# A spectral layer and a two-level mixture of experts on one core: rows of a pair in half tiles, two buffers for z tiles and weights, one hand-given order for early and main jobs

## The chip, the cores and the metric

One Trainium2 chip, one of its cores. The metric is device microseconds of one launch. The kernel before took 1245.92 us, the median of three runs from 1244.65 to 1246.6.

## The reference

`x` has 8 batches of 1856 positions and 256 channels. Each batch goes through a Fourier layer, and each of the 14848 resulting rows through one of 16 small networks, chosen in two levels.

```python
X = np.fft.rfft(x, axis=1);  Xr, Xi = X.real, X.imag
Yr = Xr @ w_r - Xi @ w_i + b_r
Yi = Xr @ w_i + Xi @ w_r + b_i
Y  = shrink(Yr) + 1j * shrink(Yi)          # sign(v) * max(|v| - 0.01, 0)
y  = np.fft.irfft(Y, n=1856, axis=1).reshape(14848, 256)

g  = argmax(y @ w_group);      e = argmax(y @ w_expert[g])     # 4 groups of 4 experts
out[row] = softmax_g * softmax_e * (relu(y @ w1[g, e]) @ w2[g, e])   # 256 -> 1024 -> 256
```

## The kernel before, in words

**Numbers.** fp32 operands are split into a high and a low fp32r part, and a product is three matmuls: high by high, high by low, low by high. The high part is a copy on ACT, the low part a subtraction on DVE. So nearly every matmul on PE waits for an ACT step and a DVE step.

**Spectral part.** The batches go in four pairs (0 to 3). 1856 = 29 x 64, so a transform is a DFT over 29, a DFT over 64 with its twiddles, and on the way back the same in reverse. A pair's spectrum stands in a "z tile" (`zys[pr]`, 32 KB per partition), its output rows in a row tile (`vs[pr]`, 128 partitions x 32 rows x 260 numbers: 256 channels, a row id and the gate).

**Routing.** For each half of a pair (16 rows per partition) PE computes 20 logits per row (`g_mm`), and a chain of small DVE steps (`route_g`) finds the expert, the gate, and the slot in that expert's list. The 32 rows per partition then go to the lists in DRAM (`xs_d`) by 32 indirect DMAs, the scatters: they are issued on POOL (L274), and the next one waits until the one two before it has landed (`FLY = 2`).

**Experts.** Eight *early jobs* (`EJOBS`: experts 0 to 3, two lists of 256 rows each) run while the last pair is finished; their rows are fetched as soon as the pairs before have been scattered. Their weights come through the staging tiles `xt` and are split into an 8192-number weight tile. Then come the *main jobs* (`JOBS`) for the rest of each list, with rows fetched by `fetch` (L435, L294 and L295 for the row ids and gates), prepared by `prep` (L446, L449, L450) and multiplied by `up_g` (L462 to L468) and `down_g` (L516, L517). A row's result is stored by an indirect DMA on POOL (L503).

**What sets the order.** PE, ACT and DVE run in the order in which the program emits their instructions (`tc.manual_schedule`). Up to the end of the early jobs this order is a string, `ORDER`, in which each letter emits the next instance of one step; DMAs go to SP's and POOL's queues in the same order. The letters that matter here, with the engine:

- `l` loads a piece of x of pairs 2 and 3 or of an early expert's weights (SP, L570 and L575); `c` first DFT (PE, L581); `d` transpose into the z tile (DVE, L343); `e` second DFT (PE, L595); `f g i` copies and signs (ACT), `h` remainder (DVE, L613); `j` bias (ACT); `k` the complex linear layer, 24 matmuls (PE, L638); `m n` two relus (ACT, L645); `o` their difference into the z tile (DVE, L651), which ends the forward work of a pair;
- `p q` high and low part (ACT L549, DVE L553), `r` first inverse DFT (PE, L320), `s` 16 transposes per pair into the row tile (DVE, L677); `t u` high and low part of rows, `v` second inverse DFT (PE), `w` its result back into the row tile (ACT, L700), `x` rows turned (PE, L708), `y z` copies into a `yt` tile (ACT or DVE, L714), `G` gate logits (PE, L731), `H` their transpose (DVE, L739), `R` one routing step (DVE), `S` one scatter (POOL, L274);
- `W V` split of an early expert's weights (ACT L760, DVE L765), `F` fetch of early rows (SP, L774), `I` their ids, `T X Y` turned and split (PE, ACT L790, DVE L795), `U` first layer (PE, L807), `A B` relu and remainder (ACT L814, DVE L818), `D` second layer (PE), `E J` gating (ACT L836, DVE L841), `K` the store (POOL, L503).

**Buffers.** The pool `big` has three tiles of 32.5 KB per partition. z tiles, row tiles, x of pair 1, and the split weights of the early and main jobs take turns in them; whoever takes a tile waits for the last reader of what stood there. So a pair's first `s` (which takes a tile) waits until an older row tile or z tile is done with.

**The two schedules.** `ORDER` is emitted inside one `manual_schedule`, the main jobs inside a second one. Between them the pools of the main jobs are opened (`xq`, `yp`, `hq`, two PSUM pools, `ft`) and the table of flexible jobs is begun.

Of the kernel before, what the change touches and what calls it, by code (L numbers as in the profile page):

```python
# [31 lines left out]
K1 = 15  # L32
# [30 lines left out]
RRSkRRhSidRdfkdgShnmioSjRcRnRcmRRSjclRokRRSdddScncmdojcSdeldSfehgcfihSgcidcdcSdkdlSeSnkmfoSgjhieSnkmfoSgjhpipe
qSmqkfghSpiqpneqSmojkfSghnijoeSmknfojghiemrnrfsgjrsrpspepskphiqqrqmqrsfgrsprpsepnskpjhiqqrqfqgrsprpsrpsepskhiq
qrqfqgrsrsrseskhtioutmuetovtumuvwvwxtwxuyzxtvtzuvwutvwuvwtvwuxwxyxyxyxtzGtzuGtufvHgvnRRwvuRwhvRwRRjeRRwRxRixtR
RxtukRtRRRtRRRyRRyRRyvfgxuwRzRnvRjGRwRRkRRRShiuuvSfovwhmeowSxmxzgyeSinxxnojzmSzcjoGndSjcoHcRRdSRcRdclRdScRRcdR
RcdSRklRRRdSRRRRRRRRSkmRRnfdjShgcmocSndcfojghReSdiiRcdRScRlRcRRkSRRdddScmcnSdfkojldgShiemSnkfojShgiemSnkfojShg
# [88 lines left out]
def spectral_moe(ctx: ExitStack, tc: tile.TileContext, x, wri, bri, wgate, w1, w2, cst, out):  # L156
# [4 lines left out]
    big = ctx.enter_context(tc.tile_pool(name="big", bufs=3))  # L161
# [52 lines left out]
    def route_g(pr, L, r0, n):  # L214
# [47 lines left out]
        for r in range(n):  # L262
            pend.append((pr, sloti[:, r:r + 1], vs[pr][:, r0 + r, :]))
# [37 lines left out]
    inv = ctx.enter_context(ExitStack())  # L301
# [900 lines left out]
```

## Time and profile before

| what | value |
|---|---|
| three runs, median (lowest to highest) | 1245.92 us (1244.65 to 1246.6) |
| the profiled execution, its own time | 1245.95 us |
| its span in the trace | 1243.8 us |
| mean granted clock of PE | 0.983 |
| busy: PE, PE weight loads | 1182.3 us (95%), 1018.1 us (82%) |
| busy: DVE, ACT, POOL | 750.3, 670.1, 255.3 us |
| early and spectral part, main jobs | 580.6, 663.2 us of the span |

PE, PEld (its weight loads, beside the matmuls), DVE, ACT and POOL are engines; SPq is SP's DMA queue. In a timeline row stand the start and the duration in us, engine, line, operation, out<-in by the program's tile names, and in brackets the us that the engine waited just before it and what ended that wait. `big` in a row is whatever tile of that pool the line uses. In a row of waits stand the engine, tile and line that waited, what released it, the us waited, the number of waits and the longest one. A busy share is an average over stages with different limits, so the stages are read one by one.

### The profile page before, as it was taken

What the parts mean: (1) busy time and instruction counts of PE and PEld (TensorE: products, weight loads), DVE (VectorE), ACT (ScalarE), POOL (GpSimd) and SP (SyncE); (2) the same over time, 40 slices, a digit from 0 to 9 for tenths busy, and PEclk for the clock granted to TensorE, in tenths of its full rate; (3) what the DMA queues carried; (4) which work ended last, traced back from release to release, by engine and by line L of the source; (5) the groups of instructions that cost most, each with busy time, mean ns of one, the idle gap of its engine ahead of it and who ended that gap; (6) DMA issues with size and microseconds to landing.
All of it is one profiled execution on the core that took longest, in us unless ns stands there. A gap on an engine that the chain in (4) does not pass through costs nothing.

```text
span 1243.8 us, 20312 instructions
## 1 busy us (share of the span) xinstructions
PE 1182.3 (95%) x7418; PEld 1018.1 (82%) x7418; DVE 750.3 (60%) x1678; ACT 670.1 (54%) x1512; POOL 255.3 (21%) x257
## 2 busy tenths in 40 slices
PE   8999999999999789939999999999999999999997
PEld 5988988886999378938879888798798888888876
DVE  4459765878598868624655645555555474474452
ACT  2876967584869266414354544445454463463442
POOL 1000054014402534541101111111111211211111
PEclk9999999999999999979989999999999999999999
DMA  9870034005100243431325345345243345346200
GB/s 382 338 291 23 2 111 143 9 13 185 65 1 21 75 163 120 162 117 41 120 102 174 120 167 179 108 138 212 83 148 120 116 165 188 108 143 226 95 13 28
DMA packets 38629, 155.89 MB, mean 125 GB/s; under 512 B 7285, under 2 KB 9466, under 8 KB 28032
## 3 DMA queue, kind: packets, MB, share of 16 engines
q1 hardware_dynamic: 19648, 104.45, 24.1%
q0 software_dynamic: 12048, 30.67, 6.8%
q10 hardware_dynamic: 6832, 19.46, 4.0%
q8 instruction: 59, 0.97, 0.3%
q14 instruction: 42, 0.34, 0.1%
HBM read 104.60 MB, written 52.46 MB: 126 GB/s over the span
## 4 chain that ended last, share of the span: by engine, by line
PE 80%; ACT 5%; DMA 4%; issue 4%; DVE 4%; POOL 1%; POOLq 0%; SPq 0%; DVEq 0%; ACTq 0%
PE ph L462 21%; PE py L516 15%; PE pw L638 11%; PE py L517 8%; PE bank L320 6%; PE pg L595 3%; PE bank L581 2%; PE ph L807 2%; PE bank L708 2%; DMA big<-in_x_dram 2%; PE pg L446 2%; PE ph L481 2%; DMA xs_d<-big,sloti 1%; PE bank L731 1%; PE ph L1040 1%
## 5 line engine op out<-in xcount | busy, mean ns | idle before, releaser
L516 PE MATMUL py<-big,hh 128*128 128x512 f32 x824 | 298.5, 402 | 0.0
L462 PE MATMUL ph<-xth,big 128*128 128x384 f32 (+1 forms) x896 | 256.4, 361 | 2.0 <-DVE yo L841 1.1
L503 POOL DMA_INDIRECT out_dram<-yo,si x123 | 121.2, 985 | 596.6 <-DVE yo L524 515.2
L517 PE MATMUL py<-big,hl 128*128 128x256 f32 x824 | 231.8, 281 | 0.9 <-DVE hl L468 0.9
L274 POOL DMA_INDIRECT xs_d<-big,sloti x128 | 130.8, 1022 | 367.2 <-ACT yt L714 133.8
L468 DVE SCALAR_TENSOR_TENSOR hl<-ph,hh 128x256 fp32r<-128x256 f32 x448 | 151.7, 381 | 68.7 <-ACT hh L466 68.3
L516 PEld LDWEIGHTS py<-big,hh 128*128 128x128 f32 x824 | 155.0, 188 | 37.7 <-issue 3.2
L462 PEld LDWEIGHTS ph<-xth,big 128*128 128x128 f32 x896 | 165.8, 189 | 20.9 <-PE ph L462 1.8
L466 ACT ACTIVATE hh<-ph 128x256 fp32r<-128x256 f32 x448 | 134.3, 353 | 78.2 <-PE ph L462 74.4
L523 ACT ACTIVATE yo<-py,si 128x256 f32<-128x256 f32 x103 | 48.9, 475 | 218.5 <-PE py L517 218.5
L462 PE MATMUL ph<-xtl,big 128*128 128x384 f32 (+1 forms) x448 | 161.0, 359 | 0.0
L517 PEld LDWEIGHTS py<-big,hl 128*128 128x128 f32 x824 | 154.9, 188 | 1.6 <-DVE hl L468 1.5
L524 DVE SCALAR_TENSOR_TENSOR yo<-py,si,yo 128x256 f32<-128x256 f32 x103 | 49.8, 484 | 176.0 <-ACT yo L523 176.0
L638 PE MATMUL pw<-wh,xh 128*128 128x256 f32 x480 | 121.9, 293 | 0.0
L638 PE MATMUL pw<-wl,xh 128*128 128x256 f32 x480 | 115.8, 280 | 0.0
L422 DVE TENSOR_TENSOR big<-xt,big 128x512 fp32r<-128x512 f32 x168 | 114.1, 683 | 0.0
L421 ACT CAST big<-xt 128x512 fp32r<-128x512 f32 x168 | 104.1, 624 | 0.0
L638 PEld LDWEIGHTS pw<-wh,xh 128*128 128x128 f32 x480 | 90.4, 188 | 2.7 <-issue 2.1
L638 PEld LDWEIGHTS pw<-wl,xh 128*128 128x128 f32 x480 | 90.5, 189 | 1.9 <-issue 1.7
L462 PEld LDWEIGHTS ph<-xtl,big 128*128 128x128 f32 x448 | 84.7, 189 | 7.2
L553 DVE TENSOR_TENSOR sl<-big,sh 128x512 fp32r<-128x512 f32 x112 | 73.1, 693 | 18.5 <-ACT sh L549 18.2
L549 ACT CAST sh<-big 128x512 fp32r<-128x512 f32 x112 | 66.3, 626 | 22.4 <-DVE big L677 10.4
(202 smaller groups left out, 2009.1 us busy)
## 6 DMA issues: line engine op xcount, KB each, us to landing
xt<-in_w_dram SPq DMA_DIRECT2D x50, 1024.0 KB, 5.2
xs_d<-zero ACTq DMA_DIRECT2D x16, 1170.0 KB, 6.3
big<-in_w_dram SPq DMA_DIRECT2D x16, 1024.0 KB, 9.1
big<-in_x_dram SPq DMA_DIRECT2D x8, 1024.0 KB, 13.0
xt<-in_x_dram SPq DMA_DIRECT2D x8, 1024.0 KB, 5.4
xg<-xs_d SPq DMA_DIRECT2D x16, 390.0 KB, 3.2
xg<-xs_d SPq DMA_DIRECT2D x12, 520.0 KB, 4.7
xg<-xs_d SPq DMA_DIRECT2D x8, 260.0 KB, 4.1
```

Of the source, the lines that this page charges most:

```text
L274: ins = nc.gpsimd.indirect_dma_start(out=xs_d, out_offset=bass.IndirectOffsetOnAxis(ap=sl_, axis=0), in_=row, in_offset=None, bounds_check ...
L320: nc.tensor.matmul(o, lhsT=lhs[a_], rhs=rhs[b_], start=i == 0, stop=i == 2)
L421: nc.scalar.copy(out=wt[:, 2 * i, cs], in_=raws[i][:, cs])
L422: nc.vector.tensor_tensor(out=wt[:, 2 * i + 1, cs], in0=raws[i][:, cs], in1=wt[:, 2 * i, cs].bitcast(F32), op=ALU.subtract)
L462: nc.tensor.matmul(o[:, :n], lhsT=a_[:, ch, fs], rhs=b_[:, ch, 0:n], start=k == 0, stop=k == 5)
L466: nc.scalar.activation(out=hh[:, f, :m], in_=ov, func=AF.Relu)
L468: nc.vector.scalar_tensor_tensor(out=hl[:, f, :m], in0=ov, scalar=0.0, in1=hh[:, f, :m].bitcast(F32), op0=ALU.max, op1=ALU.subtract)
L503: ins = nc.gpsimd.indirect_dma_start(out=out, out_offset=bass.IndirectOffsetOnAxis(ap=ids.si[:, t:t + 1], axis=0), in_=ysb, in_offset=None ...
L516: nc.tensor.matmul(o, lhsT=hh[:, f, ts], rhs=w2b[:, :, f, :], start=f == 0, stop=f == 7, skip_group_check=True)
L517: nc.tensor.matmul(o[:, 0:D], lhsT=hl[:, f, ts], rhs=w2h[:, f, :], start=False, stop=f == 7, skip_group_check=True)
L553: nc.vector.tensor_tensor(out=lo, in0=src, in1=units[key].bitcast(F32), op=ALU.subtract)
L638: nc.tensor.matmul(y[:, bt * D:(bt + 1) * D], lhsT=a_[:, bt * 2 + ch, cs], rhs=w_[:, ri, ch, :], start=False, stop=fin, skip_group_check=True)
```

## The change

**Row tiles.** `big` has two tiles instead of three, for z tiles and weights only. The rows of all pairs live in one tile `v` of three half tiles (16 rows per partition each). A pair uses two of them: half 0 is always the first, half 1 the second for pairs 0 and 2 and the third for pairs 1 and 3. So a pair's rows come to stand on the first half of the pair before, but on the second half of the pair two before. x of pair 1 is loaded into the last two thirds of `v` before any rows are there. The transposes of step `s` therefore write two runs of 16 instead of one of 32 in a row (for odd pairs the two are not adjacent).

**Smaller tiles.** A `yt` tile holds 4 row groups instead of 8, so `G` is called 32 times instead of 16, each with eight matmuls half as wide. The hidden tiles of the early jobs hold 2 of the 8 feature blocks instead of all 8, with 6 buffers of each name for 2.

**One order.** One `manual_schedule` (`ms`) now holds both `ORDER` and the main jobs. The pools of the main jobs are opened with `reuse_waits="tile"`. Weights of main jobs take turns in `third` (a pool of one tile opened after the spectral part) and the two tiles of `big`.

**The string.** `ORDER` is a new string, 2040 letters for 2024 (16 more `G`); the steps are the same and each kind keeps its own sequence. Of its 19 lines the diff shows the last.

```diff
-AYBDSUEJUKABDASBUSUABDSABDESJDKDEJKDDEJKDEJK
+BDASBUEJSUDXSYDAASBBDEJSUUASBDASBUEJSUKDDAKABBDKDEJKDEJDKEJK
...
-    big = ctx.enter_context(tc.tile_pool(name="big", bufs=3))
+    big = ctx.enter_context(tc.tile_pool(name="big", bufs=2))
...
+    vv = vp.tile([128, 3, 16, RW], F32, name="v")
+    vs = {pr: vv[:, 0:2] if pr % 2 == 0 else vv[:, 0:3:2] for pr in range(NP)}
...
     def load_x(pr):
-        t = big.tile([128, 4, 32, 64], F32, name="big")
+        if pr:
+            t = vv.rearrange("p s r w -> p (s r w)")[:, 16 * RW:16 * RW + 8192].rearrange("p (c r d) -> p c r d", c=4, r=32)
+        else:
+            t = big.tile([128, 4, 32, 64], F32, name="big")
...
     def split_w(raws):
-        wt = big.tile([128, 4, 2048], F32R, name="big")
+        wt = next(homes).tile([128, 4, 2048], F32R, name="big")
...
     def b_turn(pr, j):
-        if j == 0:
-            vs[pr] = big.tile([128, 32, RW], F32, name="big")
-        nc.vector.transpose(out=vs[pr][:, :, j * 16:(j + 1) * 16].rearrange("p r d -> p d r"),
+        nc.vector.transpose(out=vs[pr][:, :, :, j * 16:(j + 1) * 16].rearrange("p h r d -> p d h r"),
                             in_=psum.pop(("b", pr, j)).rearrange("p (k d b) -> p d k b", k=16, b=2))
...
-        if u % 4 == 0:
-            yts[pr, u // 4] = wi.tile([128, 2, 8, 128], F32, name="yt", bufs=2)
+        if u % 2 == 0:
+            yts[pr, u // 2] = wi.tile([128, 2, 4, 128], F32, name="yt", bufs=2)
...
-    @steps_of(pairs, range(4))
+    @steps_of(pairs, range(8))
     def g_mm(pr, h):
...
-        cs = slice(h % 2 * 256, h % 2 * 256 + 256)
+        cs = slice(h % 4 * 128, h % 4 * 128 + 128)
...
-        if f == 0:
-            hid[n] = [early["hp"].tile([128, 8, 256], F32R, name=nm) for nm in ("hh", "hl")]
+        hid[n, f] = [early["hp"].tile([128, 2, 256], F32R, name=nm) for nm in ("hh", "hl")]
...
+    ms = ExitStack()
     with ExitStack() as ph:
         done = 0
-        with tc.manual_schedule(engines=engines):
-            for c in ORDER.replace("\n", ""):
-                next(steps[c])
+        ms.enter_context(tc.manual_schedule(engines=engines))
+        for c in ORDER.replace("\n", ""):
+            next(steps[c])
...
-                    early["hp"] = ph.enter_context(tc.tile_pool(name="hp", bufs=2))
+                early["hp"] = ph.enter_context(tc.tile_pool(name="hp", bufs=6))
...
+    homes = cycle((pool("third", 1), big, big))
...
-    with tc.manual_schedule(engines=engines):
+    with ms:
         prev = None
```

Lines move by one to fourteen: L274 becomes L275, L294 and L295 become L295 and L296, L450 becomes L457, L574/L575 become L581/L582, L677 becomes L685, L774 becomes L782, L795, L818 and L841 become L803, L825 and L848.

The instruction order shows where the change moves work. First DVE at the end of the early jobs. L818 and L841 are remainders and gatings of early jobs, L795 an early job's row remainder, L294 and L295 the ids of a main job's rows, L450 the remainder of its turned rows. Before:

```order
531 L818 SCALAR_TENSOR_TENSOR hl<-ph,hh 128x512
532 L294 TENSOR_SCALAR si<-xg 128x3
533 L795 TENSOR_TENSOR xtl<-pg,xth 128x512
534 L295 COPY si<-xg 128x3
535 L818 SCALAR_TENSOR_TENSOR hl<-ph,hh 128x512
536 L450 TENSOR_TENSOR xtl<-pg,xth 128x2x256
537 L818 SCALAR_TENSOR_TENSOR hl<-ph,hh 128x512 x2
538 L841 SCALAR_TENSOR_TENSOR yo<-bank,si,yo 128x256 x2
539 L450 TENSOR_TENSOR xtl<-pg,xth 128x2x128
```

The same place after:

```order
542 L803 TENSOR_TENSOR xtl<-pg,xth 128x512
543 L825 SCALAR_TENSOR_TENSOR hl<-ph,hh 128x512 x2
544 L848 SCALAR_TENSOR_TENSOR yo<-bank,si,yo 128x256
545 L825 SCALAR_TENSOR_TENSOR hl<-ph,hh 128x512 x2
546 L848 SCALAR_TENSOR_TENSOR yo<-bank,si,yo 128x256
547 L825 SCALAR_TENSOR_TENSOR hl<-ph,hh 128x512 x2
548 L848 SCALAR_TENSOR_TENSOR yo<-bank,si,yo 128x256 x3
549 L295 TENSOR_SCALAR si<-xg 128x3
550 L296 COPY si<-xg 128x3
551 L457 TENSOR_TENSOR xtl<-pg,xth 128x2x256
552 L457 TENSOR_TENSOR xtl<-pg,xth 128x2x128
```

The main job's ids and row remainders (128x3, 128x2x256, 128x2x128) stood between the early jobs' last steps and now stand behind all of them.

Second, SP's queue, which issues the loads: `xt<-in_w_dram` are halves of an expert's weights, `xg<-xs_d` rows from the lists (520 numbers per partition for an early job, 780 for a main job). Before:

```order
13 L575 DMA xt<-in_w_dram 128x2048 x2
14 L774 DMA xg<-xs_d 128x520 x7
15 L575 DMA xt<-in_w_dram 128x2048 x2
16 L774 DMA xg<-xs_d 128x520
17 L575 DMA xt<-in_w_dram 128x2048 x4
18 L409 DMA xt<-in_w_dram 128x2048
19 L435 DMA xg<-xs_d 128x780
```

And after:

```order
12 L582 DMA xt<-in_w_dram 128x2048 x2
13 L782 DMA xg<-xs_d 128x520
14 L582 DMA xt<-in_w_dram 128x2048 x2
15 L782 DMA xg<-xs_d 128x520 x6
16 L582 DMA xt<-in_w_dram 128x2048 x2
17 L782 DMA xg<-xs_d 128x520
18 L582 DMA xt<-in_w_dram 128x2048 x2
19 L416 DMA xt<-in_w_dram 128x2048 x2
20 L442 DMA xg<-xs_d 128x780 x3
```

The second expert's weights stood behind seven fetches of early rows and now stand behind one; the first main weights (L416) stand ahead of the first main rows as two, where one was ahead before.

Third, DVE where the steps `s` of pair 1 begin (L677, then L685), with `q` (L553, then L560), `h` (L613, L620), `o` (L651, L658) and pair 2's `d` (L343, L350) around them. Before:

```order
173 L677 STREAM_TRANSPOSE big<-bank 128x16x32 x4
174 L613 TENSOR_TENSOR xl<-pg,xh 128x4x128
175 L553 TENSOR_TENSOR sl<-big,sh 128x512 x4
176 L677 STREAM_TRANSPOSE big<-bank 128x16x32 x4
177 L613 TENSOR_TENSOR xl<-pg,xh 128x4x128
178 L553 TENSOR_TENSOR sl<-big,sh 128x512 x4
179 L677 STREAM_TRANSPOSE big<-bank 128x16x32 x4
```

After:

```order
163 L560 TENSOR_TENSOR sl<-big,sh 128x512 x4
164 L685 STREAM_TRANSPOSE v<-bank 128x16x2x16 x3
165 L560 TENSOR_TENSOR sl<-big,sh 128x512 x3
166 L685 STREAM_TRANSPOSE v<-bank 128x16x2x16 x3
167 L560 TENSOR_TENSOR sl<-big,sh 128x512 x4
168 L620 TENSOR_TENSOR xl<-pg,xh 128x4x128
169 L685 STREAM_TRANSPOSE v<-bank 128x16x2x16
170 L620 TENSOR_TENSOR xl<-pg,xh 128x4x128
171 L560 TENSOR_TENSOR sl<-big,sh 128x512 x2
172 L685 STREAM_TRANSPOSE v<-bank 128x16x2x16
```

The transposes have the same count and size, with their output in two pieces, and stand more singly among the other steps.

More of the change, by code (lines that the diff above doesn't have):

```diff
@@ L1 @@
 from contextlib import ExitStack
-from itertools import islice
+from itertools import cycle, islice
 import numpy as np
@@ L63 @@
[L63 to L67, printed above, removed]
@@ L229, in route_g @@
         rs = slice(r0, r0 + n)
-        nc.vector.reciprocal(out=vs[pr][:, rs, D + 1:RW], in_=se.unsqueeze(2).broadcast_to([128, n, RW - D - 1]))
+        nc.vector.reciprocal(out=vs[pr][:, h, :, D + 1:RW], in_=se.unsqueeze(2).broadcast_to([128, n, RW - D - 1]))
         yield
-        nc.vector.tensor_scalar_add(out=vs[pr][:, rs, D], in0=kc("GID")[:, rs], scalar1=float(pr * PAIR))
+        nc.vector.tensor_scalar_add(out=vs[pr][:, h, :, D], in0=kc("GID")[:, rs], scalar1=float(pr * PAIR))
         yield
@@ L262, in route_g @@
         for r in range(n):
-            pend.append((pr, sloti[:, r:r + 1], vs[pr][:, r0 + r, :]))
+            pend.append((pr, sloti[:, r:r + 1], vs[pr][:, h, r, :]))
         yield
@@ L681, in p_high @@
     def p_high(pr, u):
-        high(("p", pr, u), vs[pr][:, 2 * u:2 * u + 2, 0:D])
+        high(("p", pr, u), rows2(pr, u))
     @steps_of(pairs, u16)
     def p_low(pr, u):
-        rest(("p", pr, u), vs[pr][:, 2 * u:2 * u + 2, 0:D])
+        rest(("p", pr, u), rows2(pr, u))
     @steps_of(pairs, u16)
@@ L743, in route_steps @@
             for h in range(2):
-                yield from route_g(pr, logits[pr, h], h * 16, 16)
+                yield from route_g(pr, logits[pr, h], h)
             if pr == NP - 3:
@@ L827, in down_mm @@
         for f in range(half * 4, half * 4 + 4):
-            last.append(nc.tensor.matmul(o, lhsT=hid[n][0][:, f, ts], rhs=w2b[:, :, f, :], start=f == 0, stop=f == 7,
-                                         skip_group_check=True))
-            nc.tensor.matmul(o[:, 0:D], lhsT=hid[n][1][:, f, ts], rhs=w2h[:, f, :], start=False, stop=f == 7,
+            hh, hl = hid[n, f // 2 * 2]
+            nc.tensor.matmul(o, lhsT=hh[:, f % 2, ts], rhs=w2b[:, :, f, :], start=f == 0, stop=f == 7, skip_group_check=True)
+            nc.tensor.matmul(o[:, 0:D], lhsT=hl[:, f % 2, ts], rhs=w2h[:, f, :], start=False, stop=f == 7,
                              skip_group_check=True)
@@ L853, in spectral_moe @@
         Y=e_low, U=up_mm, A=up_high, B=up_low, D=down_mm, E=down_act, J=down_add, K=down_out)
+    ms = ExitStack()
     with ExitStack() as ph:
         done = 0
[L857 to L867 removed]
+        ms.enter_context(tc.manual_schedule(engines=engines))
+        for c in ORDER.replace("\n", ""):
+            next(steps[c])
+            done += c == "o"
+            if c == "o" and done == NP * K1:
+                fwd.close()
+                early["mp"] = ph.enter_context(tc.tile_pool(name="mp", bufs=1))
+                yp.append(ph.enter_context(tc.tile_pool(name="yp", bufs=3)))
+                early["hp"] = ph.enter_context(tc.tile_pool(name="hp", bufs=6))
+                early["pp"] = ph.enter_context(tc.tile_pool(name="pp", bufs=2, space=PSUM))
+                early["py"] = ph.enter_context(tc.tile_pool(name="py", bufs=1, space=PSUM))
         assert not pend and all(next(g, None) is None for c, g in steps.items() if c not in "yzS")
@@ L1011, in half_load @@
     def half_load(k):
-        wt = big.tile([128, 4, 2048], F32, name="big")
+        wt = next(homes).tile([128, 4, 2048], F32, name="big")
         starts = []
```

80 lines of the change are left out of this document (41 added, 39 removed).

## The prediction

> **What bounds the kernel now.** I read the stages first: busy time of each engine between the places where one pair's forward work ends and the next stage begins (columns: stretch in us and its length, busy us and instructions of PE, PEld, DVE, ACT, POOL, then granted clock, DMA share, GB/s).
>
> ```profile
> span 1243.8 us, 20312 instructions
> ...
> 22.50:87.60 65.10, 64.86 (x498) 60.05 (x499) 26.74 (x41) 47.81 (x92) 0.00 (x0) 1.00 0.82 320
> 87.60:204.00 116.40, 115.03 (x830) 97.53 (x829) 89.36 (x166) 81.74 (x160) 23.30 (x24) 1.00 0.25 85
> 204.00:315.30 111.30, 107.32 (x790) 91.75 (x789) 86.30 (x161) 76.42 (x150) 28.73 (x29) 1.00 0.21 70
> 315.30:408.80 93.50, 89.02 (x729) 82.57 (x728) 75.40 (x143) 73.44 (x145) 21.62 (x22) 1.00 0.08 29
> 408.80:457.80 49.00, 43.77 (x238) 28.79 (x239) 39.02 (x65) 23.81 (x46) 24.29 (x24) 0.93 0.27 91
> 457.80:466.50 8.70, 3.48 (x24) 3.01 (x22) 2.66 (x10) 2.65 (x6) 0.39 (x1) 0.81 0.77 299
> 466.50:529.50 63.00, 62.67 (x472) 57.61 (x472) 46.30 (x107) 33.06 (x65) 30.08 (x28) 0.97 0.42 141
> 529.50:549.00 19.50, 0.56 (x3) 0.19 (x1) 2.45 (x7) 1.94 (x4) 11.70 (x12) 0.64 0.36 123
> 549.00:580.60 31.60, 31.55 (x205) 28.99 (x205) 10.67 (x21) 8.76 (x17) 5.85 (x6) 0.95 0.19 68
> 580.60:1243.80 663.20, 644.51 (x3576) 557.68 (x3576) 359.55 (x945) 316.33 (x825) 106.03 (x108) 0.99 0.37 129
> ```
>
> Two things stand out. From 580.6 on, the main jobs keep PE busy (644.5 of 663.2), and the change leaves them as they are. Before that there are 580.6 us in which PE is mostly busy but with two holes: 457.8 to 466.5 (3.5 us busy of 8.7, clock 0.81) and 529.5 to 549.0 (0.6 of 19.5, clock 0.64). The waits of PE up to 582 us name what ended them:
>
> ```profile
> PE ph L807 <- DVE xtl L795: 15.5, 1, 15.5
> PE bank L708 <- ACT big L700: 5.5, 2, 5.3
> ...
> PE ph L807 <- DVE hl L818: 3.5, 1, 3.5
> ```
>
> The timeline of the larger hole shows who held DVE:
>
> ```profile
> 530.82 0.47 ACT L836 ACTIVATE yo<-bank,si 128x256 f32<-128x256 f32 x1 [3.43 <-DMA out_dram<-yo,si]
> ...
> 542.07 0.98 POOL L274 DMA_INDIRECT xs_d<-big,sloti  x1 [0.30 <-issue]
> ...
> 544.66 0.33 SPq L435 DMA_DIRECT2D xg<-xs_d  x1
> ...
> 548.23 0.17 DVE L294 TENSOR_SCALAR si<-xg 128x3 int32<-128x3 f32 x1 [15.22 <-DMA xg<-xs_d]
> 548.31 0.68 DVE L795 TENSOR_TENSOR xtl<-pg,xth 128x512 fp32r<-128x512 f32 x1
> ...
> 549.05 0.58 PE L807 MATMUL ph<-xtl,big 128*128 128x256 f32 x1 [15.54 <-DVE xtl L795]
> ...
> 551.35 0.41 PE L807 MATMUL ph<-xth,big 128*128 128x256 f32 x1
> ```
>
> si<-xg 128x3 is the index step of the first **main** job (three row groups; the early jobs have two). It waits for rows that are fetched only once the last scatter (542.07) has landed, and it stands in DVE's queue ahead of the split (L795) and the relu remainders of early jobs whose data are there. DVE sits still for 15.2 us with early work behind it, and PE with it.
>
> The smaller hole is a load that left late:
>
> ```profile
> 452.80 2.72 SPq L774 DMA_DIRECT2D xg<-xs_d  x6
> 455.62 1.06 SPq L575 DMA_DIRECT2D xt<-in_w_dram  x2
> ...
> 463.85 1.66 ACT L760 CAST big<-xt 128x512 fp32r<-128x512 f32 x3 [6.06 <-DMA out_dram<-yo,si]
> ```
>
> SP issues the second early expert's weights after six fetches of early rows, and those wait for pair 2's scatters. ACT reaches the split of these weights at 457.8 and starts at 463.85; the releaser named is a store, but this cast needs the load issued at 455.62. The copies of pair 3 behind it on ACT are what PE waits for (L700, 5.3).
>
> **The change part by part.** *One hand-given order through early and main jobs.* In the new program all of DVE's early work stands ahead of the first main index step. The 15.5 us go. The 3.5 us ahead of them come from ACT waiting 3.43 for a staging buffer whose store is in POOL's queue between scatters; that can come back, so I count half. Restarting was slow: ten L807 starts from 549.05 to 551.35 take 2.30 us, 0.23 each, where PE's usual distance is 0.1175 (48 of L638 in 5.64, below), so 1.1 more. Together 15.5 + 1.7 + 1.1 = 18.3 gained. The Trainium skill, "TensorE: Matmul & The Clock Gate", Part 1, has the array at half clock after an idle window, until some 3.4 us of work have passed; by that the restart would cost about 1.7 (an estimate from the page) and the sum below would be 0.6 larger; the row's 1.1 is used.
>
> What is late next: the first main job's preparation, formerly done between early matmuls, now follows the last early matmul.
>
> ```profile
> 552.41 0.59 ACT L449 CAST xth<-pg 128x512 fp32r<-128x512 f32 x1 [19.66 <-PE pg L446]
> ...
> 553.04 0.69 DVE L450 TENSOR_TENSOR xtl<-pg,xth 128x512 fp32r<-128x512 f32 x1 [3.38 <-ACT xth L449]
> ```
>
> Cast 0.59, remainder 0.69 and the remainder of the third row group (half as wide, 0.4) leave PE some 1.7 us of waiting; before it waited about 0.7 less there. Its rows must be there too: from 542.07 (last scatter) to 548.23 (rows used) are 6.2 us. By the terms here the early jobs end at about 580.6 - 32 = 549, so scatters that end no sooner than before cost 1 to 2 more. I take +3 for the boundary (1 to 8).
>
> *SP's order.* In the new order the second expert's weights are issued ahead of the six fetches. The hole of 8.7 - 3.5 = 5.2 goes; I take 5 (2 to 5.2; a load can still be late, never earlier than its buffer).
>
> *The order string.* All letters are the same steps, differently mixed. For each piece of 40 letters I added up each engine's time, and took the largest engine per piece, averaged over where the pieces begin. A letter of DVE or ACT costs its group's mean; one of PE its matmuls times their distance in an unbroken run. Rows that carry most of it (groups by line: count, busy us, mean ns, idle before; chain: start, us, count):
>
> ```profile
> 42.55 5.64 PE pw L638 x48
> ...
> 251.83 3.67 PE bank L320 x30
> ...
> L677 DVE STREAM_TRANSPOSE big<-bank 128x512 f32<-128x512 f32 x48 | 48.2, 1122 | 7.8 <-DMA xs_d<-big,sloti 7.7
> L645 ACT ACTIVATE rn<-pw,nlam,CF 128x512 f32<-128x512 f32 x60 | 46.9, 785 | 15.0 <-PE pw L638 11.4 <-DVE big L343 3.4
> L553 DVE TENSOR_TENSOR sl<-big,sh 128x512 fp32r<-128x512 f32 x112 | 73.1, 693 | 18.5 <-ACT sh L549 18.2
> ```
>
> So one k (24 matmuls) is 2.82 us of PE, one s 1.12 of DVE, one q 0.69. Up to the last forward step of pairs 0, 1, 2, 3, the sheet gives 62.2, 123.1, 116.7, 103.3 for the old string, in all 405.3; the four stages above took 65.1 + 116.4 + 111.3 + 93.5 = 386.3. For the new string it gives 69.8, 110.1, 106.7, 106.2, in all 392.8. The difference of 12.5, at 386.3/405.3, is 11.9 gained (0 to 14; pieces of 20 or 80 letters give 14 and 10). For the rest of the string it gives 144.8 and 146.6: 1.8 lost.
>
> *Half tiles.* A pair's 16 transposes into its rows (s) now need only the first 16 scatters of the pair before, but the new string puts s close behind them. How fast POOL scatters, beside loads of x (first rows) and in a stretch where DVE has nothing but transposes (last two, nine distances apart):
>
> ```profile
> 185.75 0.97 POOL L274 DMA_INDIRECT xs_d<-big,sloti  x1 [1.64 <-DVE big L343]
> 189.46 0.97 POOL L274 DMA_INDIRECT xs_d<-big,sloti  x1 [2.73 <-DMA xs_d<-big,sloti]
> 190.74 0.98 POOL L274 DMA_INDIRECT xs_d<-big,sloti  x1 [0.30 <-issue]
> 195.48 0.97 POOL L274 DMA_INDIRECT xs_d<-big,sloti  x1 [3.77 <-DMA xs_d<-big,sloti]
> ...
> 201.21 0.97 POOL L274 DMA_INDIRECT xs_d<-big,sloti  x1 [3.48 <-DMA xs_d<-big,sloti]
> ...
> 414.87 0.97 POOL L274 DMA_INDIRECT xs_d<-big,sloti  x1 [4.94 <-DMA xg<-xs_d]
> ...
> 429.21 0.98 POOL L274 DMA_INDIRECT xs_d<-big,sloti  x1 [0.30 <-issue]
> ```
>
> Undisturbed, one takes (429.21 - 414.87)/9 = 1.59 us, and a load of x adds about 3. From a pair's first scatter to the next pair's first s the new string holds 32.3, 27.5 and 33.7 us of PE letters, some 10% more in real time: 36, 30, 37. Sixteen scatters and a landing of about 2.6 (544.66 less 542.07) need 28, plus 12 for four loads of x in pair 0 and 3 for one in pair 1: 40, 31, 28. DVE waits 4 + 1 + 0; I take 5 (0 to 15). Behind the waiting s on DVE stand the splits that PE's next matmuls need, so it counts in full. For odd pairs the transpose writes two pieces of 16 instead of 32 in a row; the nearest rows are 1122 ns (these) and 704 (the forward transposes), so 32 of them cost 0, at most 32 x 0.42 = 13 more, the other way as much less; I take 0, since the element count is the same.
>
> *Smaller yt, hidden tiles, pools.* Gate matmuls come in twice as many calls, half as wide:
>
> ```profile
> 449.21 0.59 PEld L731 LDWEIGHTS bank<-yt,wg 128*32 128x32 f32 x16
> 449.22 1.07 PE L731 MATMUL bank<-yt,wg 128*32 128x256 f32 x16
> ```
>
> Sixteen calls of 1.07 become 32 that take between 0.53 (half) and 1.07 (no shorter); loading alone is 0.59, so 0.6: +2 (0 to 17). Hidden tiles of a quarter the length and the pools' waits by tile are counted at nothing: casts and copies keep their sizes, and the third weight home is written beside the first job's matmuls; uncovered, one split is 8 casts of 0.6, 5 us.
>
> **Sum**, against the profiled execution (1245.95, its span 1243.8 and 2.15 around it; the median shown is 1245.92): -18.3 + 3 - 5 - 11.9 + 1.8 + 5 + 2 = -23.4, so **1222.5 us**.
>
> **The rivals.** *Only the holes go*: the new mixture saves nothing in the pairs' stages, because their waits are latencies from step to step that a sheet of sums cannot see. For it: the old sheet misses single stages by up to 10 us. Against: it misses in one direction in three of four. 1222.5 + 11.9 = 1234.4.
>
> *More than the sheet*: with s and the scatters side by side the stages of pairs 1 to 3 come close to PE's own letters (276.6 of 323.0 in the new sheet), and no scatter is waited for. Of that gap of 46.4 the forecast takes 11.9; another third, 15.5, on top, and the other terms as they are, give 1222.5 - 15.5 = 1207, and without half of the boundary's 3 about **1206**.
>
> *The scatters become the bound* (slower). DVE stands at the first s of pairs 1 to 3 until sixteen scatters have landed. At the 3.1 us each of 185.75 to 201.21 (five distances) sixteen take 49, 52 with the landing; against 36, 30, 37 that is 16 + 22 + 15 = 53 us, 48 more than counted: about 1271. It decides from some 2.2 us per scatter on, where the waits (0.6 x 16 x 3 = 29 more) eat the gain. Against it: the slow rows stand beside x loads, and 1.59 was kept while DVE transposed without a break. The Trainium skill, "SBUF — State Buffer", the section on two separate sides, speaks for it: a vector instruction with two SBUF inputs and a GpSimd one that reads SBUF lock each other out of a shared port, so scatters beside q and u would slow down; the 1.59 does not show it, but no stretch here has scatters beside q and u throughout.
>
> *The wait moves to the boundary*: POOL falls 10 us further behind in the tail, where scatters and stores share its queue, and PE waits there for the first main rows: 1222.5 + 10 = 1232.5. Against: POOL was busy 30.1 of 63 us at 466.5 to 529.5.
>
> **How the numbers follow.** Forecast 0.54, only the holes 0.20, more 0.15, boundary 0.05, scatters 0.06. The forecast's own range is 1213 to 1231. For 8 in 10 the range reaches into both neighbours, without the slower case: from 1206 to the 1234.4 of the holes alone with the boundary at its upper bound (8 for 3, so 5 more), **1206 to 1239**. A measurement of this kernel tells about 0.2% (2.5 us) from no change. All cases but the scatters lie far below 1243: faster 0.93, within 0.2% 0.02 (scatters a little slow), slower 0.05.
>
> **What would show it.** Right: no DVE wait of 15 us at L295 while early remainders are behind it; the first main matmul at about 552 to 560 instead of 581.6; no ACT wait at L768 for the second expert; pair stages summing to about 375 to 380; waits of L685 for scatters of 5 us in all. Wrong: waits of L685 above 9 us per pair, or PE waits between the last early and the first main matmul that add up to what went.

## The result, and the profile after

The changed kernel takes **1216.63 us** (median of four runs, 1214.89 to 1219.47) against 1246.1 us before: a ratio of 0.9768, 95% interval 0.9747 to 0.9788, or 29.5 us less. The forecast was 23.4 less, 1222.5, in a range of 1206 to 1239.

The stages of the changed kernel, cut at the same places as those of before (last forward step of each pair, then the tail, in two pieces, up to the last matmul of the early jobs; columns as before):

```profile
span 1214.9 us, 20820 instructions
...
22.30:96.90 74.60, 74.58 (x547) 66.94 (x548) 32.75 (x50) 49.20 (x96) 0.00 (x0) 1.00 0.72 282
96.90:202.10 105.20, 104.82 (x833) 90.87 (x831) 83.99 (x156) 77.71 (x152) 15.32 (x16) 1.00 0.24 84
202.10:305.20 103.10, 101.72 (x828) 90.28 (x829) 81.39 (x153) 77.96 (x151) 35.88 (x33) 1.00 0.18 61
305.20:404.90 99.70, 97.09 (x829) 89.18 (x827) 80.57 (x152) 75.17 (x146) 34.24 (x32) 1.00 0.17 61
404.90:470.50 65.60, 61.31 (x475) 45.69 (x475) 54.95 (x114) 38.33 (x75) 23.32 (x23) 1.00 0.40 138
470.50:552.50 82.00, 76.62 (x524) 70.16 (x525) 43.37 (x88) 30.94 (x60) 40.59 (x40) 0.98 0.35 122
552.50:1214.90 662.40, 643.75 (x3583) 559.08 (x3581) 360.85 (x951) 316.94 (x827) 105.71 (x108) 0.99 0.37 130
```

The four pair stages are 74.6 + 105.2 + 103.1 + 99.7 = 382.6 long, 3.7 less than before; single ones moved by up to 11 us against each other. The tail (408.8 to 580.6 before) is 171.8 - 147.6 = 24.2 shorter. The main jobs are 0.8 shorter. So the gain lies in the tail, where the two holes were: the row of 82.0 us has 5.4 idle, where 457.8 to 549.0 of before had 24.5. PE's busy time in the tail fell too, from 142.0 to 137.9: the granted clock was 0.93, 0.81, 0.97, 0.64 and 0.95 in the five rows of before, and is 1.00 and 0.98 here.

PE's waits up to 560 us. The 15.5 and the 5.3 are gone, and no wait took their place but one of 3.1; the main jobs' first matmul waits 0.7 and 0.3:

```profile
PE ph L815 <- DVE hl L825: 4.6, 3, 3.1
PE ph L681 <- DVE big L658: 2.4, 1, 2.4
...
PE ph L469 <- ACT xth L456: 0.7, 1, 0.7
...
PE ph L469 <- DVE xtl L457: 0.3, 1, 0.3
```

How the early jobs hand over to the main jobs (timeline, the engine after the duration):

```profile
530.34 0.97 POOL L275 DMA_INDIRECT xs_d<-v,sloti  x1 [0.30 <-issue]
...
553.09 0.48 DVE L848 SCALAR_TENSOR_TENSOR yo<-bank,si,yo 128x256 f32<-128x256 f32 x1 [2.35 <-ACT yo L843]
553.49 0.16 DVE L295 TENSOR_SCALAR si<-xg 128x3 int32<-128x3 f32 x1
...
552.38 0.82 PE L453 MATMUL pg<-K,xg 128*128 128x128 f32 x6
553.93 0.45 PE L469 MATMUL ph<-xth,big 128*128 128x384 f32 x1 [0.73 <-ACT xth L456]
```

The last scatter is issued 23 us ahead of the index step (L295), so the rows have long been there: the step runs without a wait, and the boundary costs PE 1.0 us.

The transposes into the half tiles, and the first, sixteenth and last scatter of pair 0 beside the first transpose of pair 1 (groups by line, then timeline):

```profile
L685 DVE STREAM_TRANSPOSE v<-bank 128x512 f32<-128x512 f32 x48 | 48.9, 1110 | 0.1
```

```profile
167.18 1.12 POOL L275 DMA_INDIRECT xs_d<-v,sloti  x1 [145.95 <-DVE big L658]
...
201.69 1.23 POOL L275 DMA_INDIRECT xs_d<-v,sloti  x1 [0.30 <-issue]
...
205.90 3.01 DVE L685 STREAM_TRANSPOSE v<-bank 128x512 f32<-128x512 f32 x3
...
228.63 0.97 POOL L275 DMA_INDIRECT xs_d<-v,sloti  x1 [0.31 <-issue]
```

48 transposes waited 0.1 us in all, and took 1110 ns each (1122 before, when the 16 pieces of 32 were in one row). The sixteenth scatter was issued 4.2 us ahead of the transpose that needs it landed; for pairs 1 and 2 that distance is 8.1 and 11.2 us.

### The profile page after: what moved, and what is told of

It is laid out like the page before. It is cut to its first block, busy times and chain, and to the rows that moved or that the text cites. A ratio compares the mean times of both kernels' runs of the same rounds, so it can differ in the third digit from the quotient of the medians.

```text
span 1214.9 us, 20820 instructions
## 1 busy us (share of the span) xinstructions
PE 1178.9 (97%) x7674; PEld 1021.8 (84%) x7674; DVE 749.7 (62%) x1680; ACT 670.4 (55%) x1510; POOL 258.4 (21%) x257
## 3 DMA queue, kind: packets, MB, share of 16 engines
q1 hardware_dynamic: 19648, 104.45, 24.2%
## 5 line engine op out<-in xcount | busy, mean ns | idle before, releaser
L275 POOL DMA_INDIRECT xs_d<-v,sloti x128 | 134.4, 1050 | 343.5 <-DVE big L658 177.9
L658 DVE TENSOR_TENSOR big<-rp,rn 128x512 f32<-128x512 f32 x60 | 42.0, 706 | 46.8 <-ACT rp L652 39.3
L602 PEld LDWEIGHTS pg<-CF,big 128*128 128x128 f32 x480 | 62.3, 196 | 8.2 <-issue 3.0
```

Source lines behind the costliest of these rows:

```text
L275: ins = nc.gpsimd.indirect_dma_start(out=xs_d, out_offset=bass.IndirectOffsetOnAxis(ap=sl_, axis=0), in_=row, in_offset=None, bounds_check ...
L602: nc.tensor.matmul(o[:, m * 128:(m + 1) * 128], lhsT=zys[pr][:, k, ch * 128:(ch + 1) * 128, bt], rhs=T_v[:, k, :], start=True, stop=True)
```

## The experiments

Each median stands beside the old kernel's in the same set of runs (1246.0, 1247.7 and 1246.6 in the three sets). These differ by up to 1.6 us, so a difference between kernels of two sets is no finer than that.

| kernel | median us | ratio to before | 95% interval |
|---|---|---|---|
| old, one schedule | 1236.9 | 0.9925 | 0.9898 to 0.9951 |
| old, loads ahead | 1242.0 | 0.9958 | 0.9942 to 0.9974 |
| old, both | 1230.7 | 0.9871 | 0.9845 to 0.9897 |
| old, both, small hidden tiles | 1230.3 | 0.9868 | 0.9849 to 0.9887 |
| old, both, small hidden tiles, 8 staging buffers | 1224.9 | 0.9810 | 0.9783 to 0.9836 |
| old, halved yt tiles | 1256.7 | 1.0087 | 1.0070 to 1.0104 |
| changed, two schedules | 1228.5 | 0.9850 | 0.9827 to 0.9874 |
| changed, old string (overwrites rows, see below) | 1258.2 | 1.0081 | 1.0057 to 1.0105 |
| changed, 5 staging buffers | 1218.3 | 0.9760 | 0.9732 to 0.9789 |
| changed, 1 scatter on its way | 1320.6 | 1.0572 | 1.0538 to 1.0606 |
| changed, 3 scatters | 1205.8 | 0.9677 | 0.9662 to 0.9693 |
| changed, 3 scatters, 5 staging buffers | 1206.4 | 0.9683 | 0.9667 to 0.9698 |

**One schedule, on the old kernel.**

```diff
+    ms = ExitStack()
...
-        with tc.manual_schedule(engines=engines):
+        ms.enter_context(tc.manual_schedule(engines=engines))
...
-    with tc.manual_schedule(engines=engines):
+    with ms:
```

> The kernel before with one change: one manual schedule holds its old order string and the main jobs, so the main job's index step stands behind the early jobs' work on DVE. Theory (the gain is the two holes of PE): the 15 us wait goes and nothing comes in its place, since in the changed kernel PE waited only 1.0 us ahead of its first main matmul: 1246 - 18 = 1228 (1224 to 1232). Rival (the new string is what lets the wait go; with the old one it moves to the boundary, because the last scatter lands at 543 and the rows behind it at 548): early work ends about 562, rows are there at 548, so even this rival can hold back little of it; it gives 1236 or more only if stores and scatters fall further behind.

It won 9.1 us, half of what was expected. The theory fell; the rival's figure came, but not its place, since PE waits 1.0 us at the boundary. The stretch of the tail in which PE now stands still, and what ACT and POOL do ahead of it:

```profile
538.80:548.10 9.30, 2.84 (x17) 2.21 (x15) 1.76 (x4) 2.25 (x5) 3.77 (x5) 0.83 0.74 255
```

```profile
524.49 0.97 POOL L274 DMA_INDIRECT xs_d<-big,sloti  x1 [0.30 <-DMA xs_d<-big,sloti]
...
536.89 0.97 POOL L274 DMA_INDIRECT xs_d<-big,sloti  x1 [0.30 <-issue]
538.16 0.97 POOL L503 DMA_INDIRECT out_dram<-yo,si  x1 [0.30 <-issue]
...
540.72 0.97 POOL L503 DMA_INDIRECT out_dram<-yo,si  x1 [0.30 <-issue]
...
540.68 0.47 ACT L836 ACTIVATE yo<-bank,si 128x256 f32<-128x256 f32 x1 [5.14 <-DMA out_dram<-yo,si]
546.32 0.47 ACT L836 ACTIVATE yo<-bank,si 128x256 f32<-128x256 f32 x1 [5.16 <-DMA out_dram<-yo,si]
```

Nine scatters in a row (524.49 to 536.89) stand in POOL's queue ahead of the stores (L503), and ACT's gated copies (L836) wait twice 5 us for a staging buffer (`yo`) whose store is among them. The relus and casts of the next early job stand behind these copies on ACT. This wait had been covered by DVE's wait for the main rows; with that gone it is the one that ends last.

In the profiled execution the early jobs end at 567.0, 13.6 us sooner than before, and the main jobs take 3.8 longer (667.0 for 663.2): PE's waits in them are nearly the same, but its granted clock was 0.93 in their first 73 us and in their last 74, for 0.95 and 0.96 before. And PE's 5.3 us wait for L700, the smaller hole, is only 1.6 here (0.9 and 0.7), though this edit does not aim at it; so the 9.1 is not the price of the larger hole alone.

**The loads ahead of the fetches, and both edits.**

```diff
...
+        if n == 1:
+            for i in range(2):
+                tc.add_manual_dep(ins.ins, wload[1, i].ins.name, ahead, reason="order on the queue")
```

> The kernel before with one change: the second early expert's two weight loads are issued on SP ahead of the six fetches of early rows, all else as it was. Theory: the hole of 5.2 us of PE goes: 1241 (1240 to 1243). Rival (what is won there is waited for again at the larger hole, which ends when the last scatter has landed whatever happened before): 1246, no change.

> The kernel before with both edits: one manual schedule, and the second expert's loads ahead of the fetches. Theory (the two holes are most of the gain): 1246 - 18 - 5 = 1223 (1220 to 1227), which leaves 6 us of the measured 29.5 to the new string and the half tiles. Rival (string and half tiles carry half of it): 1230 or more.

The loads alone won 4.0 (interval 3.2 to 7.2), and 6.2 on top of the one schedule; PE's 5.3 us wait for L700 is gone in both. Together the two holes gave 15.4 of the 29.5, not 23. The rival's figure for both ("1230 or more") is what came, so nearly half of the gain has to come from elsewhere.

**Two schedules, on the changed kernel.**

```diff
+        ms.close()
         assert not pend and all(next(g, None) is None for c, g in steps.items() if c not in "yzS")
...
-    with ms:
+    with tc.manual_schedule(engines=engines):
```

> The changed kernel with one part undone: two manual schedules again, so that the first main job's index step is back among the early jobs' steps on DVE. Theory (the wait is as long as the last scatter is late against DVE): DVE reaches that place at about 531, the last scatter is issued at 530.3 and the rows are there some 6 us later, so DVE stands for 5 to 6 us, of which 3 are waited for in the changed kernel anyway: 1217 + 3 to 6 = 1220 to 1223. Rival (the wait costs its old 15 to 18 us whenever the step stands there): 1232 to 1235.

11.9 lost, between the two. Timeline of this kernel, the last scatter, the fetch and PE:

```profile
533.98 0.97 POOL L275 DMA_INDIRECT xs_d<-v,sloti  x1 [0.30 <-issue]
...
536.63 0.84 SPq L442 DMA_DIRECT2D xg<-xs_d  x2
...
539.72 1.12 PE L453 MATMUL pg<-K,xg 128*128 128x128 f32 x4 [11.98 <-DMA xg<-xs_d]
```

The expectation looked at DVE alone. PE's own transposes of the main rows (L453) come forward too, PE reaches them at 527.7, and the last scatter is 3.6 us later than in the changed kernel. That the price is set by how late the last scatter is against the first engine that needs its rows holds; the place was read off wrongly.

**Staging buffers, and the small hidden tiles by themselves.**

```diff
...
-                    yp.append(ph.enter_context(tc.tile_pool(name="yp", bufs=3)))
-                    early["hp"] = ph.enter_context(tc.tile_pool(name="hp", bufs=2))
+                    yp.append(ph.enter_context(tc.tile_pool(name="yp", bufs=8)))
+                    early["hp"] = ph.enter_context(tc.tile_pool(name="hp", bufs=6))
```

> The old kernel with one schedule and the early loads, and besides with eight staging buffers for the early jobs' outputs instead of three; to make room the hidden tiles are the small ones of the changed kernel. Theory (what takes the place of the 15 us wait is ACT's wait for a staging buffer whose store stands in POOL's queue among the scatters; PE's 7.2 us of it go): 1230.7 - 7 = 1224 (1222 to 1226). Rival (the time is set by when scatters and stores end, so it comes back ahead of the main jobs): 1229 to 1231.

> The old kernel with one schedule, the early loads and the small hidden tiles, but three staging buffers: the part of the last experiment on the old kernel that isn't the staging. Theory (the 5.8 us won there were ACT's waits for a staging buffer): 1230.7, as without the small tiles (1229 to 1232). Rival (the gain was the hidden tiles, six short ones for two long ones): 1225.

With eight buffers 1224.9, with three 1230.3: the hidden tiles are worth 0.4, which is within the noise, the staging 5.4 (6.5 if each run is taken against the old kernel of its own set). ACT's waits in the tail (500 to 562 us) with three buffers:

```profile
ACT yo L841 <- DMA out_dram<-yo,si: 16.0, 5, 6.8
```

With eight this row is gone. So the wait for a store was the second wait behind the first, and five more kilobytes per partition of staging took it away without any new order. What that is worth rests on the medians: in the profiled execution, the longest of the five (1228.4), PE's longest wait behind these steps falls from 5.0 to 2.6, but PE waits 2.6 for L703 earlier, and the tail is only 1.2 shorter (152.3 for 153.5).

**The halved yt tiles, on the old kernel.**

```diff
-        if u % 4 == 0:
-            yts[pr, u // 4] = wi.tile([128, 2, 8, 128], F32, name="yt", bufs=2)
+        if u % 2 == 0:
+            yts[pr, u // 2] = wi.tile([128, 2, 4, 128], F32, name="yt", bufs=2)
...
```

> The old kernel with the halved yt tiles alone: 32 gate calls half as wide for 16, each extra one behind the second of its four copies. Theory (from the distances of PE's starts, a pair's gate matmuls take 4.7 us for 4.0, 3 us over four pairs, and nothing waits for them): 1246 + 3 = 1249 (1247 to 1250). Rival (the gate then follows closely behind its copies and PE waits for them, as in the run of the changed kernel with the old string, where PE waited 5.3 us there): 1251 to 1257.

10.1 lost; the rival's figure. Its stages of pairs 1, 2, 3:

```profile
87.40:207.50 120.10, 117.46 (x893) 99.10 (x892) 89.22 (x164) 81.99 (x160) 22.48 (x23) 1.00 0.24 82
207.50:322.90 115.40, 109.92 (x855) 93.42 (x854) 86.37 (x162) 77.18 (x151) 30.80 (x29) 1.00 0.20 68
322.90:421.50 98.60, 91.97 (x793) 84.24 (x791) 75.45 (x143) 74.12 (x145) 22.61 (x23) 1.00 0.08 29
```

They are 3.7, 4.1 and 5.1 us longer than before, of which PE's busy time takes 2.4, 2.6 and 3.0. The gate's own matmuls are 2.7 of these 8.0; where the other 5.3 come from was not followed. The tail, 168.3 for 171.8, gives 3.5 back. The gate's matmuls in this kernel, and below in the changed one:

```profile
L731 PE MATMUL bank<-yt,wg 128*32 128x128 f32 x512 | 20.4, 278 | 5.4 <-DVE yt L714 2.6 <-ACT yt L714 2.6
```

```profile
L739 PE MATMUL bank<-yt,wg 128*32 128x128 f32 x512 | 20.6, 279 | 0.6 <-ACT yt L722 0.6
```

The matmuls themselves cost the same in both. In the old string PE waits 5.4 us right behind the copies; the new string puts the gate where the copies are done, and waits 0.6.

**The old string in the changed kernel.** The diff shows the line with the first gates (`G`); 16 gate letters are added to the old string and nothing else.

```diff
-otcutcutdfvdgvmhwcuwuvtdtvwuxwuvyviwxwxyxyGyxtGyxuteyuvttGuwvutxnukwzjotuxfvgzhmkwtiunjxoGfzgvHmvRRwvhRwRxRtRx
+ztfughnxixfzGvghyvwtvwxuwxyxyGyGtvtvuwutewxutxyeuyvinGwtxHvmRRyvowRvuwRRxtRwRxRRyGkRyRtRRutRRjRRRxmRRvRyRRvfwG
...
```

> The changed kernel (half tiles, small tiles, one schedule) with the old order string, into which only the 16 extra gate letters are put, each behind the second of its four copies; SP then issues the second expert's weights behind the fetches again. Theory (tiles and buffers by themselves are worth nothing; the 14 us between the old kernel with both holes mended, 1230.7, and the changed kernel come from the new string): as the old kernel with one schedule, 1237 (1234 to 1240). Rival (the half tiles by themselves free what the pairs' stages waited for): 1226 or less.

In the old string only 10 of pair 2's scatters stand ahead of pair 3's first transpose (16 to 21 for each pair in the new one), so rows 10 to 15 of each partition of pair 2 go out partly with pair 3's values; nothing in this kernel keeps them until they are sent. It moves as much data as the others and is 10.5 slower than before, and 21 slower than the old kernel with one schedule: both theories fell, since the new tiles under the old string cost a good deal. DVE's waits in its tail (400 to 470 us):

```profile
DVE v L685 <- DMA xs_d<-v,sloti: 15.1, 5, 3.4
```

Pair 3's transposes wait 15.1 us for pair 2's scatters, and the gate's matmuls wait 5.5 us, as above. Tiles and string are one edit: the half tiles are paid for unless the order keeps scatters and gates at a distance.

**Staging in the changed kernel.**

```diff
-                yp.append(ph.enter_context(tc.tile_pool(name="yp", bufs=3)))
+                yp.append(ph.enter_context(tc.tile_pool(name="yp", bufs=5)))
...
-        xgs[n] = xg = early["mp"].tile([128, 2, RW], F32, name="xg", bufs=6)
+        xgs[n] = xg = early["mp"].tile([128, 2, RW], F32, name="xg", bufs=5)
```

> The changed kernel with five staging buffers for the early jobs' outputs instead of three; five buffers for fetched rows instead of six make the room. Theory: the one PE wait of 3.1 us that begins with ACT's wait for a store, and its slow restart, go: 1216.6 - 4 = 1213 (1211 to 1215). Rival (the wait stands beside others, or the fifth row buffer is missed): 1216 to 1219.

1218.3 (1214.6 to 1222.8): no gain, the rival. ACT waits for no store any more in the tail, but PE waits 1.9 us at L794 for early rows, whose fetches left at 443.7 (437.1 in the changed kernel). The row buffer that was given up is not shown to be the cause: the kernel with two schedules has six and waits 2.5 there, and the one with three scatters and five row buffers (below) does not wait. The profiled execution was one of the longer ones (1222.3), with pair stages 2.1 longer than the changed kernel's, so this run doesn't price the staging alone.

**One and three scatters on their way.**

```diff
-FLY = 2
+FLY = 1
```

> The changed kernel with one scatter on its way at a time instead of two. Theory (a pair's transposes follow closely behind the first sixteen scatters of the pair before): in the changed kernel pair 0's first fifteen distances took 34.5 us, 2.3 each, and the sixteenth had landed only some 2 us before the first transpose. One at a time, a scatter takes its issue of 1.0, some 2.6 to land and 0.3: 3.9 each, sixteen take 62; DVE waits some 20 to 25 us in pairs 1 to 3 each, and the tail is later too: 1217 + 60 to 85 = 1277 to 1302. Rival (the scatters have room): under 1240. If the first is so, the slower case of the prediction was real in kind and only not reached.

104 lost. First and last scatter of pair 0, and DVE's waits:

```profile
167.29 1.12 POOL L275 DMA_INDIRECT xs_d<-v,sloti  x1 [145.90 <-DVE big L658]
...
274.67 0.97 POOL L275 DMA_INDIRECT xs_d<-v,sloti  x1 [1.70 <-DMA xs_d<-v,sloti]
```

```profile
DVE v L685 <- DMA xs_d<-v,sloti: 54.8, 3, 20.6
```

(274.67 - 167.29)/31 = 3.5 us per scatter, and the first transposes of pairs 1 to 3 wait 54.8 in all. The pair stages are 40.8 us longer than in the changed kernel (445.7 for 404.9), the tail 40.5 (188.1 for 147.6) and the main jobs 23.2 (685.6 for 662.4). In the last two PE waits for early rows and for the first main rows:

```profile
PE pg L794 <- DMA xg<-xs_d: 24.5, 1, 24.5
```

```profile
PE pg L453 <- DMA xg<-xs_d: 23.6, 1, 23.6
```

The slower rival of the prediction is real in kind, and its 53 us of waits are near the measured ones (at 3.1 us per scatter, for 3.5 here). Its time, 1271, left out what late scatters cost behind the pairs. The changed kernel is free of these waits by some 1.6, 5.5 and 8.6 us in pairs 0, 1 and 2, if a landing takes the prediction's 2.6.

```diff
-FLY = 2
+FLY = 3
```

> The changed kernel with three scatters on their way at a time instead of two. Theory (in the changed kernel no transpose waits for a scatter, and the tail's stores stand between scatters in POOL's queue only as far as these wait): 1216.6 less at most the 3 us of PE's wait that begins at a store: 1213 to 1217. Rival (the scatters still set the pairs' pace by delaying what is queued behind them): 1205 to 1212.

> The changed kernel with three scatters on their way and five staging buffers (five buffers for fetched rows). Theory: with earlier scatters the rows fetched through the fifth buffer and the stores are both earlier, so the 3.1 us wait, its slow restart and the 1.9 us wait for rows that the run with five staging buffers showed all go: 1212 (1210 to 1214). Rival (the remaining waits are steps that follow each other, not buffers): 1215 to 1218.

Three scatters on their way give **1205.8 us**, 10.9 less than the changed kernel and 3.2% less than before (interval 3.1 to 3.4): the best kernel here. The theory fell; the rival's figure came, but not its place, since the pair stages end only 1.1 earlier. In this kernel the first and last scatter of pair 0 are issued at these times, and the stretch of the tail up to the last early matmul is this:

```profile
167.19 1.12 POOL L275 DMA_INDIRECT xs_d<-v,sloti  x1 [145.91 <-DVE big L658]
...
219.47 0.98 POOL L275 DMA_INDIRECT xs_d<-v,sloti  x1 [0.30 <-DMA xs_d<-v,sloti]
```

```profile
403.80:541.90 138.10, 134.86 (x1000) 114.42 (x1001) 97.93 (x201) 70.20 (x136) 64.54 (x63) 1.00 0.40 139
```

ACT's waits for a staging buffer in the tail, first of the changed kernel, then of this one:

```profile
ACT yo L843 <- DMA out_dram<-yo,si: 8.0, 2, 5.7
```

```profile
ACT yo L843 <- DMA out_dram<-yo,si: 1.0, 1, 1.0
```

A scatter takes (219.47 - 167.19)/31 = 1.7 us for (228.63 - 167.18)/31 = 2.0 in the changed kernel. The pair stages end 1.1 earlier (403.8 for 404.9), the tail is 147.6 - 138.1 = 9.5 shorter: PE's idle time in it falls from 9.7 to 3.2, and its busy time by 3.1, of which 1.6 are the slow stretch of the last section below, which is gone (granted clock 1.00). PE's wait of 3.1 is gone too. Two more staging buffers, with one row buffer fewer, then add nothing (1206.4). Three scatters in the old kernel weren't tried.

## Why the prediction was right, and where it was not

The sum was 6 us short, and that it came so near is in part luck. The two holes were forecast at 18.3 + 5 = 23.3 and gave 15.4 on the old kernel. All the rest was forecast at 3 - 11.9 + 1.8 + 5 + 2 = -0.1, so at nothing, and gave the other 14.0 (1230.7 less 1216.6). The mechanism of the holes was right; both sizes were off, in opposite ways.

**The stall: 18.3 expected, 9.1 measured.** The step that failed is "that can come back, so I count half", on the 3.5 us that ACT waits for a staging buffer. It came back whole and larger: once DVE's wait was gone, the stores behind the scatters ended last, and PE lost 6.5 of 9.3 us there, 4.7 more than the 1.8 that the sum left. Another 3.8 were lost in the main jobs, where the sum has no term. Undone in the changed kernel the schedule is worth 11.9; that the new order has less of the second wait (3.1 us of PE) is the likely reason, and no run shows it by itself.

**The boundary: +3 expected.** PE waits 1.0 us there, and waited about as long in front of its first main matmul before; nothing was lost. The last scatter was issued at 530.3, where the prediction had scatters end "no sooner than before" (542).

**SP's order: 5 expected, 4.0 and 6.2 measured.** Right in size.

**The order string: 11.9 expected in the pair stages, 3.7 measured,** with the halved yt tiles in it. The sheet promised more than there was idle time: the four rows quoted in the prediction hold 64.86 + 115.03 + 107.32 + 89.02 = 376.2 us of busy PE in 386.3, so 10.1 idle. That is no hard bound, since matmuls can also follow each other more closely: PE's letters for pairs 1 to 3 add up to 276.6 in the prediction's new sheet, and PE is busy 303.6 there in the changed kernel. The order did little of that. After, PE is busy 378.2 of 382.6: 5.7 us of the idle time went, and 2.0 more of busy time, with 192 more gate matmuls in it, took part of that back. The sheet got the shifts between stages right (its four differences +7.6, -13.0, -10.0, +2.9; measured +9.5, -11.2, -8.2, +6.2).

**The rest of the string: 1.8 lost expected; it won.** From the old kernel with both holes mended (1230.7) to the changed kernel are 14.0 us. In the profiled executions the pair stages end at 410.3 and 404.9, the last early matmul at 564.3 and 552.5, the span at 1228.5 and 1214.9: 5.4 in the pair stages, 6.4 in the tail, 1.8 in the main jobs. The split is rough: with the old string unchanged the pair stages end between 408.8 and 410.3 in the profiled executions, with the new one (two scatters on their way) between 404.9 and 407.0. In the tail eight staging buffers alone would win about as much (5.4, above). The new string does it by order: its stores stand earlier among the last pair's scatters, and ACT waits 8.0 us for a staging buffer in place of 16.9. That reading is by the order of POOL's queue and by the waits; no run moved the stores alone, and none has the new string without the half tiles or without the new pools of the main jobs.

**Half tiles: +5 expected, 0.1 measured.** The estimate of 40 us for pair 0's sixteen scatters against 36 of PE's work was close: 34.5 to the issue of the sixteenth, so some 37 with a landing of 2.6, and 38.7 to the first transpose. The margin was on the other side by 2 us, and the run with one scatter shows what lies beyond it. The two-piece transposes cost nothing, as taken.

**Gate matmuls: +2 expected.** Busy time 20.6 for 16.9, so +3.7, and 0.6 of waits: twice the term, and well inside its bounds (0 to 17). In the old order it cost 10.1. Small hidden tiles: nothing clear of the noise, as taken.

**The rivals.** "Only the holes go" named 1234.4; the holes by themselves give 1230.7. "More than the sheet" named 1206 by a better mixture; it takes three scatters on their way to get there. The wait did not move to the boundary; with one scatter on its way it does (23.6). It moved to the stores, which the prediction had seen as 3.4 us of ACT's waiting and not followed further.

**Its signs.** DVE's 15 us wait is gone, the first main matmul starts at 553.9, and L685 waits 0.1: as named, or better. The pair stages sum to 382.6, a little above the 375 to 380. ACT does wait at L768 for the second expert, 13.4 us up to 424.1; the releaser named is pair 3's inverse DFT (L681), which reads a tile of `big`, and not the load. No wait of PE names this one.

## What to carry to other kernels

When an engine's long wait is taken away, look at each wait that it covered, one queue further: here DVE's 15 us hid ACT's wait for stores behind scatters, and mending the first gave half. Before trusting a sheet of costs, add up the idle time of the engine that bounds the stage: it was 10.1 us here, and the order won 5.7 of it. Where indirect transfers share a queue with work that others wait for, try how many may be on their way before building orders around them: one constant was worth 10.9 us. And add up a forecast by its causes, not only by its total: this one was near by two errors that nearly cancelled.

## What the runs showed of the hardware

PE's granted clock can fall some time after a pause. In the changed kernel PE stands for 3.1 us, from 532.2 to 535.3; the matmuls then start at full rate and slow down later (timeline, then the stretch in the columns of the stages, with the clock at 0.53):

```profile
535.27 0.39 PE L815 MATMUL ph<-xth,big 128*128 128x256 f32 x1 [3.10 <-DVE hl L825]
...
536.20 0.28 PE L815 MATMUL ph<-xtl,big 128*128 128x256 f32 x1
...
536.54 0.28 PE L815 MATMUL ph<-xtl,big 128*128 128x256 f32 x1
...
538.38 0.41 PE L815 MATMUL ph<-xtl,big 128*128 128x256 f32 x1
...
539.02 0.41 PE L815 MATMUL ph<-xtl,big 128*128 128x256 f32 x1
```

```profile
536.50:540.10 3.60, 3.60 (x19) 3.50 (x19) 1.25 (x3) 1.02 (x2) 0.97 (x1) 0.53 0.22 78
```

Three matmuls take 0.34 us up to 536.5, 1.3 us after the restart, and 0.64 from then to 540.1. By the Trainium skill, "TensorE: Matmul & The Clock Gate", Part 1, the throttle works in windows of about 3.4 us that run free of the program; the 3.4 us at half rate here agree with that length. A window that ended only then would explain the delay, but no run shows a window by itself. The prediction named a whole idle window; here a pause of 3.1 us came before the fall. The price, 1.6 us, comes on top of the wait.

A scatter's issue on POOL takes 0.97 us as a rule, and 1.4 to 1.5 in two of these rows, beside DVE's subtractions of two SBUF tiles (L560; the changed kernel's timeline):

```profile
203.61 1.41 POOL L275 DMA_INDIRECT xs_d<-v,sloti  x1 [0.69 <-DVE xl L620]
205.32 1.50 POOL L275 DMA_INDIRECT xs_d<-v,sloti  x1 [0.30 <-issue]
207.21 0.97 POOL L275 DMA_INDIRECT xs_d<-v,sloti  x1 [0.38 <-ACT sh L556]
...
203.49 2.49 DVE L560 TENSOR_TENSOR sl<-big,sh 128x512 fp32r<-128x512 f32 x4
```

The prediction cited the Trainium skill, "SBUF — State Buffer", the section on two separate sides, for a lock between the two. The rows agree in kind: of the changed kernel's 128 scatters, the 57 that run beside hardly any DVE step with two SBUF inputs (under 0.1 us of overlap) take 0.97 to 1.12 us, the others up to 1.73, though many of them take 0.97 as well. That a lock is the reason no run shows. It is too small to set the pace. With one scatter on its way none of the 114 that follow another scatter leaves POOL right behind it (0.30 us); with two 51 of 121 do, with three 100 of 122, and the period of pair 0's scatters is 3.5, 2.0 and 1.7 us.
